# An mLSTM and two expert layers on one core: the first phase in finer steps and a new order of its first 520

## The chip, the cores and the metric

The program runs on one core of a Trainium2 chip. The metric is the device time in microseconds (us) of one execution; lower is better. The engines are TensorE (PE in the rows; PEld is its weight load), VectorE (DVE), ScalarE (ACT), GpSimd (POOL) and SyncE (SP), which issues nearly all DMAs from one queue in order.

## The reference

```python
for t in range(S):                      # attention: B, H, S, D = 4, 8, 768, 40
    m_new = max(f_gate + m, i_gate)
    f_stab, i_stab = exp(f_gate + m - m_new), exp(i_gate - m_new)
    C = f_stab * C + i_stab * outer(v, k)
    n = f_stab * n + i_stab * k
    y = sigmoid(o_gate) * (C @ q) / max(abs(n . q), 1)
h = x @ w_in                            # x: 3072 x 320, w_in: 320 x 2048
x = (max(h, 0) + alpha * min(h, 0)) @ w_out
e = argmax(x @ w_gate)                  # 8 experts, 320 -> 1024 -> 320
out = prob[e] * sigmoid(x @ w_output_gate)[e] * relu(x @ w1[e]) @ w2[e]
```

## The kernel before

The recurrence is computed in chunks of 128 tokens: 24 units u (4 batches of 6 chunks). For each unit `load_g`, `att_e`, `att_s` build the decayed scores, `att_h` the part from the running state, `att_b` the sum over values, `att_y` the normalised and gated output y, `att_c` its transpose into the FFN's input `xT`, and `prep_kt` and `att_d` update the state. Three units make one block of 384 tokens, and the dense FFN goes over 8 blocks with 16 chunks of 128 hidden columns each: `ffn1` k (eight matmuls of 384 columns into the PSUM tile `ph`, then ScalarE's `v` and VectorE's scaled sum), `ffn_split` k (the activation as a high part on ScalarE and the rest `gl` on VectorE, into the tile `ring`), `ffn2` k (nine matmuls of 336 columns into `acc`). `block_out` reads `acc` after the sixteenth.

All matmul operands are kept in two parts, a rounded high part and the rest. So the weights are decoded and split at the start: `load_wi`, `dec_wi` (three VectorE instructions, L614 to L618, that put 64-bit words together as float32), `split_wi` (L630 on ScalarE, L631), and `load_wo`, `dec_wo`, `split_wo` (L647, L648) likewise, 16 of each; `gate_w` and `gate_w2` multiply `w_out` by the router's weights with small matmuls (`pw`, `pwg`). `gates` makes the gate prefix sums `G` of a part of the sequence in nine VectorE instructions and stores them to the DRAM tensor `gd`, from which `load_g` broadcasts them back as `D`; `gates_e` and `gates_d` turn them into factors (`pe_ek`, `pe_dec`). `expert_load`, `expert_split` and `expert_store` prepare the experts' weights for the second layer, which runs from about 500 us on.

Everything up to the second layer stands in one written order: the string ORDER has a code for each step (F is `ffn1`, g `ffn_split`, S `ffn2`, as `att_s`, and so on; STEPS maps them), and each engine's queue gets the instructions as the steps come. No scheduler changes this afterwards, and an engine whose next instruction waits holds all behind it. The table OTHER says for which numbers of a step the elementwise instruction goes to the other of VectorE and GpSimd: `engine(usual, other, name, i)`. ORDER also has 20 `warm` steps, each one 512-column matmul on zeros whose result nothing reads (L1172).

PSUM tiles come from three tags: `att` (3 buffers, attention and `pw`, `pwg`), `acc` (3) and `hps` (2, the `ph` tiles). `v` comes from a pool with 2 buffers.

Of the kernel before, what the change touches and what calls it, by code (L numbers as in the profile page):

```python
# [8 lines left out]
F32 = mybir.dt.float32  # L9
# [8 lines left out]
P = 128  # L18
# [25 lines left out]
KR = 64 + D  # L44

OTHER = {
    "prep_kt": (
        1, 3, 4, 7, 8, 9, 13, 14, 15, 16,  # L50
    ),
    "att_y": (
        0, 1, 2, 4, 7, 11, 13, 16, 17, 18, 19, 20, 21, 22, 23,
    ),
    "expert_split": (
        0, 1, 2, 3, 5, 6, 7, 8, 10, 12, 13, 14, 15, 18, 19, 20, 25, 26, 27, 30, 31, 32, 33, 34, 35, 36,
        37, 38, 39, 40, 41, 42, 43, 44, 45, 46, 47, 48, 49, 50, 51, 52, 53, 54, 55, 56, 57, 58, 59, 60,
        61, 62, 63,
    ),
    "split_wi": (  # L60
        0, 1, 3, 5, 13, 14,
    ),
    "split_wo": (
        2, 4, 10, 15,
# [5 lines left out]
for _n, _w in (  # L70
# [11 lines left out]
lo load_gates do load_cst load_gates lo lo gates do gates_e lq gates gates_e do do warm ah so load_g ae gw do do so  # L82
do do gw load_wg load_sel li gates_d gates_d lv pt lv di di di si gv gv do lo do do do load_g ae as lg ad so so log
sg li li gw gw lq li di di di di load_g ab ay pt ay load_g di load_gates si ah ay ay di si ad ae di di di ac lo do
warm warm si load_g load_g do gv ae as ae lo lq do do do do warm ab ay so so ay ay gv ay gw warm lo lo lo warm warm
warm lg gw do ae do do do so as do lv ac gv lq lq ah gates ab set_al1 gv ay gw lo do do gw warm warm so li pt do
warm lg warm warm gates_e do so load_g ay ay ay warm do do gates_d gw di do di warm warm di lv ac warm warm warm ad
pt si el load_g es li di di lo gv gv F di load_g F g et ah si ae do g lo do do ae S F gw as so so load_g warm g S
gw do do li di log do so ae li di ad di lv gv gv F gw di di di ae F as lg load_g ah si lo si g do do ae g S S lg lg
li do so di ab ay ay ay pt di el es lq gw di li di log F F di di et g g ad si pt li di li di di si di di sg gv lo  # L90
lq sg si el S S load_g ay F F g S di ah do lv ab si do load_g do es li et F g gv li lv ay ac ay lo ay ay di g S S
ae ae di as so gw di di di F F ab di g g si li lv ac load_g di ay si S di load_g load_g li gv do di S ay el do ay
do ay F gv ae si F g di di S ae S pt lg lo g lq lq di as el ae si ad so ad pt F ac load_g do g do do ab ay ay S so
gw gw es ah log ay et ay F gv gv g lg es F g as S ah F F g ab et load_g S ae g load_g ae ay ay ay el ad bo el el es
es F F lg load_g ae S ac load_g lv ae S pt et g S g es ah lq lv ad F ay g F S as lq ah F et ab ay S g g ac el ay et
es lv el F F as S g es load_g ae lg lg et ay lq ay S sg S et g F ab ay load_g bp lg S g ac S pt el ad F F S g g S
el el es lq es F g F g ay ay ay ah pt S pt S et es F S et g F log ad g ae et as ae S bo F g F load_g ae ab ay el lv
el S g ay es el F as g load_g load_g es et es et F load_g ac lv ah el el ae ae lg lg S g S S F g ad pt ah ay es F g
ab F ay ad et ae et S g el load_g el F es ay et F ay ay ac S g es ae S g ah F S S et es ay et g lv el el bp as F F
el g es et pt S S ab ac g ad F F g S g ay lq sg es es S ay lv pt F ay el lq g F as S g F et es ah ad S log S g bo F  # L100
sg et g load_g load_g ay el el F lg S ae ab ay ay ay et S F S g lq lq S g ae ac lg el S as lv load_g load_g load_g
es et es et ay F pt F g g ab ae ay ac F S g es ay ay ay S F F ae as lq S g g load_g ah ad ac ae el F lv pt el ae g
et ab ay ay S es es F et et g load_g ay F S g as ay lv S load_g S F g F ah ab ay S el el es ad lg ay ae g ay el es
# [12 lines left out]
first_s first_tl route_c2 first_t first_tl first_s first_2 first_2 route_d first_st first_2 first_2
# [19 lines left out]
    "di": ("dec_wi", [(i, j) for i in range(16) for j in range(3)]),  # L136
    "gates_e": ("gates_e", zip(range(3))),
# [12 lines left out]
    "warm": ("warm", zip(range(20))),  # L150
# [31 lines left out]
def mlstm_moe_kernel(  # L182
# [262 lines left out]
    with ExitStack() as p1:  # L445
# [70 lines left out]
        def gates(part):  # L516
            c0, c1, o = GPARTS[part]
            nn, n = c1 - c0, (c1 - c0) * P
            fs = slice(c0 * P, c1 * P)
# [3 lines left out]
            gx[part] = GG, w  # L523
# [5 lines left out]
            V.tensor_tensor(g[:, 1:], tf[:, 1:], m[:, : n - 1], ALU.add)  # L529
            lo = 1 if part == 0 else 0  # L530
            V.tensor_tensor(g[:, lo:], g[:, lo:], m[:, lo:], ALU.subtract)
            V.tensor_copy(mlast, m[:, n - 1 : n])
            for c in range(nn):
                cs = slice(c * P, (c + 1) * P)
                V.tensor_tensor_scan(GG[:, cs], onesP[:GR], g[:, cs], 0.0, ALU.mult, ALU.add)
            V.tensor_tensor(w, ti, m, ALU.subtract)
            V.tensor_tensor(w, w, GG, ALU.subtract)
            nc.sync.dma_start(gd[:, fs], GG[: B * H])

        def gates_e(part):  # L540
            c0, c1, o = GPARTS[part]
            nn, n = c1 - c0, (c1 - c0) * P
            GG, w = gx[part]
            V.tensor_tensor(
# [105 lines left out]
        def gate_w(i):  # L650
# [3 lines left out]
            for k in range(3):  # L654
                c0 = min(k * P, DM - P)
                T.transpose(pt[:, k * P : (k + 1) * P], f[:, c0 : c0 + P], ident)
# [666 lines left out]
```

## Time and profile before

| | |
|---|---|
| median of 3 runs | 784.55 us (780.52 to 784.94) |
| the profiled execution | 782.92 us |
| its span, first to last instruction | 781.1 us |
| TensorE, VectorE, ScalarE, GpSimd busy | 751.7, 472.0, 363.2, 164.9 us |
| mean granted TensorE clock | 0.99 |

The profile is of one execution. Times are counted from the span's start. A matmul's end is modelled, so a busy TensorE need not be one at its peak; the distance between the starts of two matmuls is measured. TensorE's matmuls of float32 operands run in two passes, which the rows count as two instructions.

### The profile page before, as it was taken

The numbers are of one execution on the slowest core, as the hardware profiler recorded it, in microseconds if no ns is written. First come the engines' busy times: TensorE is split into PE (matmuls) and PEld (weight loads), VectorE is DVE, ScalarE is ACT, GpSimd is POOL, SyncE is SP. The second block draws the span as 40 slices with busy tenths as digits, with TensorE's granted clock in tenths as the row PEclk, the third lists the DMA queues.
The fourth block names the chain that finished last, engine by engine and source line by source line (L and its number), as shares of the span: only waits on it lengthen the run. The fifth ranks groups of instructions, "written<-read, shape, count | busy, mean of one in ns | idle before, by whom it ended". The sixth has DMA issues, their size and how long they took to land. (4 is left out here: it accounts for less than half of the span.)

```text
span 781.1 us, 15245 instructions
## 1 busy us (share of the span) xinstructions
PE 751.7 (96%) x4931; PEld 714.8 (92%) x4931; DVE 472.0 (60%) x1159; ACT 363.2 (47%) x810; POOL 164.9 (21%) x225
## 2 busy tenths in 40 slices
PE   2899999999999999999999999999999999999995
PEld 2787999989999999999999999998999999999994
DVE  4878998775767566767687786867332232232231
ACT  3536666636664654655565354433333233233231
POOL 1222433203130323210000000012232232232232
PEclk9988999999999999999999999999999999999998
DMA  6938877876788785766977868795977645921000
GB/s 194 258 111 262 271 243 231 258 234 242 230 283 296 236 294 179 234 234 245 307 255 257 294 240 303 274 340 189 383 305 292 240 171 201 428 83 39 29 22 13
DMA packets 81787, 179.64 MB, mean 230 GB/s; under 512 B 8700, under 2 KB 39481, under 8 KB 80428
## 3 DMA queue, kind: packets, MB, share of 16 engines
q1 hardware_dynamic: 78252, 169.92, 63.4%
q0 software_dynamic: 3456, 8.71, 3.3%
q8 instruction: 45, 0.74, 0.4%
q14 instruction: 34, 0.28, 0.1%
HBM read 246.55 MB, written 55.59 MB: 387 GB/s over the span
## 5 line engine op out<-in xcount | busy, mean ns | idle before, releaser
L834 PE MATMUL ph<-ring 128*128 128x384 f32 x1024 | 196.7, 340 | 0.0
L834 PEld LDWEIGHTS ph<-ring 128*128 128x128 f32 x1024 | 177.0, 188 | 1.8 <-DVE ring L850 0.4
L862 PE MATMUL acc<-ring 128*128 128x336 f32 x384 | 123.4, 326 | 0.5 <-ACT ring L849 0.5
L863 PE MATMUL acc<-ring 128*128 128x336 f32 x384 | 119.6, 317 | 0.0
L842 ACT ACTIVATE v<-ph 128x384 f32<-128x384 f32 x128 | 62.3, 489 | 114.5 <-PE ph L834 114.2
L843 DVE SCALAR_TENSOR_TENSOR ph<-v,al,ph 128x384 f32<-128x384 f32 x128 | 78.3, 618 | 53.2 <-ACT v L842 52.8
L409 DVE TENSOR_SCALAR yo<-po,xg 128x320 f32<-128x320 f32 x26 | 14.3, 551 | 137.3 <-PE po L289 137.3
L289 PE MATMUL po<-ring,hh 128*128 (+1 forms) x432 | 95.6, 308 | 0.0
L289 PE MATMUL p<-ring,xh 128*128 (+1 forms) x324 | 89.9, 398 | 0.0
L850 DVE TENSOR_TENSOR ring<-ph,ring 128x384 fp32r<-128x384 f32 x128 | 70.3, 553 | 31.4 <-ACT ring L849 29.7
L849 ACT ACTIVATE ring<-ph 128x384 fp32r<-128x384 f32 x128 | 62.1, 488 | 52.9 <-DVE ph L843 43.4
L865 PE MATMUL acc<-ring 128*128 128x336 f32 x384 | 80.2, 317 | 0.0
L289 PEld LDWEIGHTS po<-ring,hh 128*128 128x128 f32 x432 | 73.2, 187 | 2.3 <-ACT hh L389 0.2
L862 PEld LDWEIGHTS acc<-ring 128*128 128x128 f32 x384 | 72.3, 188 | 1.9 <-ACT ring L849 0.9
L863 PEld LDWEIGHTS acc<-ring 128*128 128x128 f32 x384 | 72.3, 188 | 0.0
L389 ACT ACTIVATE hh<-p 128x512 fp32r<-128x512 f32 x54 | 29.4, 595 | 86.5 <-PE p L387 86.5
L289 PEld LDWEIGHTS p<-ring,xh 128*128 128x128 f32 x324 | 58.8, 188 | 11.3
L289 PE MATMUL po<-ring,hl 128*128 (+1 forms) x216 | 66.5, 308 | 0.2 <-DVE hl L391 0.2
L376 ACT ACTIVATE hr<-p 128x512 f32<-128x512 f32 x56 | 33.4, 597 | 67.3 <-PE p L289 63.7
L865 PEld LDWEIGHTS acc<-ring 128*128 128x128 f32 x384 | 63.5, 189 | 0.2 <-DVE ring L850 0.2
L700 ACT ACTIVATE D<-D,EKT 128x128 f32<-128x128 f32 x192 | 60.7, 393 | 3.5 <-DMA D<-gd 3.3
L410 POOL DMA_INDIRECT out_dram<-yo,tok x28 | 28.1, 1003 | 160.8 <-DVE yo L409 146.2
(197 smaller groups left out, 1139.6 us busy)
## 6 DMA issues: line engine op xcount, KB each, us to landing
ring<-scr SPq DMA_DIRECT2D x26, 3072.0 KB
ring<-scr SPq DMA_DIRECT2D x26, 2560.0 KB
ring<-scr SPq DMA_DIRECT2D x33, 512.0 KB
D<-gd SPq DMA_DIRECT2D x48, 256.0 KB
er<-in_ew_dram SPq DMA_DIRECT2D x32, 384.0 KB
scr<-ring SPq DMA_DIRECT2D x32, 384.0 KB
scr<-er SPq DMA_DIRECT2D x32, 384.0 KB
er<-in_ew_dram SPq DMA_DIRECT2D x32, 320.0 KB
```

Of the source, the lines that this page charges most:

```text
L289: mm = T.matmul(o_, lhsT, r, start=start, stop=stop)
L376: A.activation(hr_half(j, hf), ph, AF.Relu)
L389: A.activation(hh[:, hs], pts[j, hf], AF.Copy)
L700: A.activation(d[:, j], d[:, j], AF.Exp, bias=EKT[:, c, i + j : i + j + 1])
L834: T.matmul(ph[:, :384], wi_[i][lo][:, wc], xTs[n % 2][:, xc], start=(a == 0), stop=(a == len(PASSES) - 1),)
L842: A.activation(v, ph[:, :384], AF.Relu, scale=-1.0)
L843: V.scalar_tensor_tensor(ph[:, :384], v, al1[:, i : i + 1], ph[:, :384], ALU.mult, ALU.add)
L849: A.activation(gh, v, AF.Copy)
L850: V.tensor_tensor(gl, v, gh.bitcast(F32), ALU.subtract)
L862: T.matmul(ac, gh[:, sl], hi, start=(i == 0), stop=False)
L863: T.matmul(ac, gh[:, sl], lo, start=False, stop=False)
L865: T.matmul(accs[n][t][:, :NO], gl[:, t * P : (t + 1) * P], hi, start=False, stop=(i == NFC - 1))
```

## The change

Steps that issued matmuls and the instructions that empty their result are cut in two: `att_s` and `att_m`, `att_h` and `att_n`, `att_d` and `att_u`, `att_b` and `att_a`, `att_c` and `att_x`, `gate_w` and `gate_c`, `gate_w2` and `gate_s`, `ffn1` and `ffn_act`; `gates` is cut into `gates`, `gates_g`, `gates_st` (the store) and `gates_w`. The first 520 steps of the new ORDER, up to the first `block_out`, are a new order of the same steps as the first 443 before; behind it the order is the old one with both halves of a step side by side. No `warm` step is left. For k below 24, `ffn_act` writes its sum over `v` in SBUF and not into `ph`, and 12 of those `ffn_split` run their subtraction on GpSimd. OTHER changes for some others.

```diff
+KEEP = 24
 OTHER = {
+    "ffn_split": (
+        0, 1, 3, 4, 5, 6, 7, 9, 15, 17, 20, 22,
+    ),
     "prep_kt": (
-        1, 3, 4, 7, 8, 9, 13, 14, 15, 16,
+        0, 1, 2, 3, 4, 7, 8, 9, 13, 14, 15, 16,
     "att_y": (
-        0, 1, 2, 4, 7, 11, 13, 16, 17, 18, 19, 20, 21, 22, 23,
+        3, 4, 6, 7, 11, 13, 16, 17, 18, 19, 20, 21, 22, 23,
     "expert_split": (
-        0, 1, 2, 3, 5, 6, 7, 8, 10, 12, 13, 14, 15, 18, 19, 20, 25, 26, 27, 30, 31, 32, 33, 34, 35, 36,
+        0, 2, 3, 5, 6, 7, 8, 10, 12, 13, 14, 15, 18, 19, 20, 25, 26, 27, 30, 31, 32, 33, 34, 35, 36, 37,
...
+    "gates_w": (
+        0, 2,
+    ),
     "split_wi": (
-        0, 1, 3, 5, 13, 14,
+        1, 5, 6, 7, 8, 9, 11, 13, 14,
     "split_wo": (
-        2, 4, 10, 15,
+        1, 3, 5, 6, 8, 9, 11, 13, 14, 15,
 ORDER = """
-lo load_gates do load_cst load_gates lo lo gates do gates_e lq gates gates_e do do warm ah so load_g ae gw do do so
+lo do lo do do do do load_gates load_cst gw so gc do lo gw gates gates_g load_gates gates_w gates_e load_wg lv do
...
-es F F lg load_g ae S ac load_g lv ae S pt et g S g es ah lq lv ad F ay g F S as lq ah F et ab ay S g g ac el ay et
+F f F f lg load_g ae S ac ax load_g lv ae S pt et g S g es ah an lq lv ad au F f ay g F f S as am lq ah an F f et
...
-    "warm": ("warm", zip(range(20))),
+    "warm": ("warm", zip(range(200))),
...
             V.tensor_tensor(g[:, 1:], tf[:, 1:], m[:, : n - 1], ALU.add)
+            V.tensor_copy(mlast, m[:, n - 1 : n])
+            gx[part] = GG, w, g, m
+
+        def gates_g(part):
...
             V.tensor_tensor(g[:, lo:], g[:, lo:], m[:, lo:], ALU.subtract)
-            V.tensor_copy(mlast, m[:, n - 1 : n])
             for c in range(nn):
                 cs = slice(c * P, (c + 1) * P)
                 V.tensor_tensor_scan(GG[:, cs], onesP[:GR], g[:, cs], 0.0, ALU.mult, ALU.add)
-            V.tensor_tensor(w, ti, m, ALU.subtract)
-            V.tensor_tensor(w, w, GG, ALU.subtract)
-            nc.sync.dma_start(gd[:, fs], GG[: B * H])
+
+        def gates_st(part):
+            c0, c1, o = GPARTS[part]
+            nc.sync.dma_start(gd[:, c0 * P : c1 * P], gx[part][0][: B * H])
+
+        def gates_w(part):
...
+            eng = engine(V, G, "gates_w", part)
+            eng.tensor_tensor(w, ti, m, ALU.subtract)
+            eng.tensor_tensor(w, w, GG, ALU.subtract)
...
                     T.matmul(pp[hf][:, j * P : (j + 1) * P], qk[r, HH + j], qk[r, j], start=True, stop=True)
+            t["pp"] = pp
+
+        def att_m(u):
+            t = ut[u]
+            pp = t["pp"]
             for hf in range(2):
                 d = t["D", hf].rearrange("p h t -> p (h t)")
                 V.tensor_tensor(d, pp[hf], d, ALU.mult)
...
+            gt[k] = ph
+
+        def ffn_act(k):
+            ph = gt[k]
+            i = k % NFC
             v = hp.tile([P, 384], F32, tag="v", bufs=2, name=f"v_{k}")
             A.activation(v, ph[:, :384], AF.Relu, scale=-1.0)
-            V.scalar_tensor_tensor(ph[:, :384], v, al1[:, i : i + 1], ph[:, :384], ALU.mult, ALU.add)
-            gt[k] = ph[:, :384]
+            g = v if k < KEEP else ph[:, :384]
+            V.scalar_tensor_tensor(g, v, al1[:, i : i + 1], ph[:, :384], ALU.mult, ALU.add)
+            gt[k] = g
...
             A.activation(gh, v, AF.Copy)
-            V.tensor_tensor(gl, v, gh.bitcast(F32), ALU.subtract)
+            engine(V, G, "ffn_split", k).tensor_tensor(gl, v, gh.bitcast(F32), ALU.subtract)
```

TensorE just ahead of the first `ffn1`, before. `pw` and `pwg` are the router products, `pt` the transpose of a unit's output, `pd` the state update, `ph` the FFN; a number behind a name is that of the tile.

```order
L656 MATMUL pw_567<-cst,f_wo_478 128x128 x3
L1172 MATMUL warm_573<-ring 128x512
L1172 MATMUL warm_575<-ring 128x512
L1172 MATMUL warm_583<-ring 128x512
L1172 MATMUL warm_587<-ring 128x512
L1172 MATMUL warm_589<-ring 128x512
L554 MATMUL pe_ek_594<-cst,w_525 128x96 x3
L1172 MATMUL warm_610<-ring 128x512
L572 MATMUL pe_dec_616<-gin,sel 120x12 x3
```

The same place on TensorE now, up to the first three `ffn1`.

```order
L592 MATMUL pe_ek_569<-cst,w_412 128x96 x3
L610 MATMUL pe_dec_580<-gin,sel 120x12 x3
L693 MATMUL pw_602<-cst,f_wo_553 128x128 x3
L693 MATMUL pw_608<-cst,f_wo_575 128x128 x3
L913 MATMUL ph_617<-ring 128x384 x8
L808 MATMUL pd_626<-kv_2_398,kt 120x123 x3
L693 MATMUL pw_635<-cst,f_wo_631 128x128 x3
L913 MATMUL ph_646<-ring 128x384 x8
L706 MATMUL pwg_663<-wgt,woT_591 128x16 x3
L808 MATMUL pd_673<-kv_3_500,kt 120x123 x3
L913 MATMUL ph_677<-ring 128x384 x8
```

No warm matmul stands between the factors and the FFN any more; one `pd` and two `pwg` that stood ahead of the first `ph` stand behind it, and the first three `ph` are no longer two together.

VectorE at the prefix sums of part 2 of the gates, before.

```order
L735 TENSOR_TENSOR hN_520<-pb_516,EKT 128x328
L524 SCALAR_TENSOR_TENSOR m_522<-gin,mlast 96x384
L528 TENSOR_TENSOR g_524<-gin,mlast 96x1
L529 TENSOR_TENSOR g_524<-gin,m_522 96x383
L531 TENSOR_TENSOR g_524<-g_524,m_522 96x384
L532 COPY mlast<-m_522 96x1
L535 SCALAR_TENSOR_TENSOR G_523<-cst,g_524 96x128 x3
L536 TENSOR_TENSOR w_525<-gin,m_522 96x384
L537 TENSOR_TENSOR w_525<-w_525,G_523 96x384
```

The end of the same place on VectorE now; the part's first scan, `m_409`, stands twenty rows ahead of L560.

```order
L764 TENSOR_TENSOR D_0_394<-ps_0_469,D_0_394 128x512
L764 TENSOR_TENSOR D_1_396<-ps_1_470,D_1_396 128x512
L652 TENSOR_SCALAR f_wo_502<-r_wo_405 128x320
L654 SCALAR_TENSOR_TENSOR f_wo_502<-r_wo_405,f_wo_502 128x320
L686 TENSOR_TENSOR ring<-f_wo_420,ring 128x320
L560 TENSOR_TENSOR g_411<-g_411,m_409 96x384
L563 SCALAR_TENSOR_TENSOR G_410<-cst,g_411 96x128 x3
L656 SCALAR_TENSOR_TENSOR f_wo_502<-r_wo_405,f_wo_502 128x320
L859 TENSOR_TENSOR pa_491<-pa_491,hN_380 128x328
```

Score products, decoding and a `wo` split now stand inside the gate chain, and the two subtractions into `w` have left VectorE.

GpSimd at the first FFN chunks, before.

```order
L678 TENSOR_TENSOR kt<-kv_3_638,EKT 128x320
L631 TENSOR_TENSOR ring<-f_wi_629,ring 128x384
L701 AFFINE_SELECT D_0_602<-D_0_602 128x512
L701 AFFINE_SELECT D_1_666<-D_1_666 128x512
L648 TENSOR_TENSOR ring<-f_wo_612,ring 128x320
```

The same place on GpSimd now.

```order
L724 TENSOR_TENSOR kt<-kv_2_398,EKT 128x320
L724 TENSOR_TENSOR kt<-kv_3_500,EKT 128x320
L669 TENSOR_TENSOR ring<-f_wi_641,ring 128x384
L935 TENSOR_TENSOR ring<-v_660,ring 128x384
L747 AFFINE_SELECT D_0_587<-D_0_587 128x512
L747 AFFINE_SELECT D_1_589<-D_1_589 128x512
L686 TENSOR_TENSOR ring<-f_wo_686,ring 128x320
L935 TENSOR_TENSOR ring<-v_690,ring 128x384
```

The L935 rows are the `gl` subtractions of the first two FFN chunks, which stood on VectorE before.

## Rows read from the trace of the kernel before

**Rows 1.** The page: busy time of each engine, share of the span, instructions
```profile
PE 751.7 (96%) x4931; PEld 714.8 (92%) x4931; DVE 472.0 (60%) x1159; ACT 363.2 (47%) x810; POOL 164.9 (21%) x225
```
**Rows 2.** Busy time by stretch; then clock, DMA share, GB/s
```profile
0.00:71.50 71.50, 53.39 (x265) 46.77 (x266) 51.57 (x143) 29.40 (x73) 15.44 (x26) 0.93 0.69 199
71.50:150.70 79.20, 78.53 (x580) 75.45 (x579) 69.48 (x162) 51.23 (x129) 27.75 (x35) 1.00 0.79 252
150.70:760.00 609.30, 607.70 (x4018) 581.81 (x4018) 346.39 (x848) 279.48 (x603) 116.20 (x159) 1.00 0.68 238
```
**Rows 3.** Waits of VectorE, 0 to 71.5 us: total, times, longest
```profile
DVE f_wo L614 <- DMA r_wo<-in_wo_dram: 3.9, 1, 3.9
DVE DEC L580 <- PE pe_dec L572: 2.4, 2, 1.5
DVE G L535 <- DMA cst<-in_consts_dram: 1.9, 1, 1.9
DVE D L713 <- PE ps L710: 1.6, 2, 1.2
DVE pa L788 <- PE pa L778: 1.4, 1, 1.4
DVE dn L797 <- PE pa L778: 1.4, 1, 1.4
```
**Rows 4.** SyncE in order of time, around 50 us: start, duration, issue
```profile
44.62 1.55 SPq L478 DMA_DIRECT2D q<-in_qs_dram  x4
57.38 0.31 SPq L538 DMA_DIRECT2D gd<-G  x1
```
**Rows 5.** Busy time by stretch (columns of rows 2), 50 to 70 us
```profile
50.00:60.00 10.00, 9.24 (x56) 8.37 (x53) 8.89 (x25) 2.47 (x8) 1.46 (x2) 0.63 0.17 54
60.00:70.00 10.00, 9.46 (x56) 7.78 (x55) 8.58 (x25) 5.15 (x12) 3.59 (x5) 0.86 0.88 257
```
**Rows 6.** TensorE in order of time: start, duration, matmuls of one line
```profile
41.14 3.58 PE L778 MATMUL pa<-kv,D 128*128 128x41 f32 x16
...
60.15 2.48 PE L1172 MATMUL warm<-ring 128*128 128x512 f32 x5
...
68.47 3.04 PE L834 MATMUL ph<-ring 128*128 128x384 f32 x16
...
89.32 1.87 PE L778 MATMUL pa<-kv,D 128*128 128x41 f32 x16
...
91.31 3.04 PE L834 MATMUL ph<-ring 128*128 128x384 f32 x16
94.19 0.80 PE L750 MATMUL pd<-kv,kt 128*120 128x123 f32 x6
```
**Rows 7.** VectorE and GpSimd by line, 0 to 150.7 us: busy, mean ns, idle before
```profile
L1101 DVE TENSOR_TENSOR er<-er,ring 128x768 fp32r<-128x768 f32 x4 | 3.8, 952 | 1.0 <-ACT ring L1100 1.0
L631 DVE TENSOR_TENSOR ring<-f_wi,ring 128x384 fp32r<-128x384 f32 x6 | 3.3, 552 | 0.9 <-ACT ring L630 0.9
L648 DVE TENSOR_TENSOR ring<-f_wo,ring 128x320 fp32r<-128x320 f32 x4 | 2.2, 539 | 0.3 <-ACT ring L647 0.3
L678 DVE TENSOR_TENSOR kt<-kv,EKT 128x320 f32<-128x320 f32 x3 | 1.9, 632 | 0.8 <-DMA kv<-in_kv_dram 0.8
L537 DVE TENSOR_TENSOR w<-w,G 96x384 f32<-96x384 f32 x1 | 0.6, 553 | 0.0
...
L631 POOL TENSOR_TENSOR ring<-f_wi,ring 128x384 fp32r<-128x384 f32 x10 | 10.1, 1014 | 13.2 <-ACT ring L630 13.2
```
**Rows 8.** TensorE by line, 0 to 71.5 us
```profile
L1172 PE MATMUL warm<-ring 128*128 128x512 f32 x19 | 9.5, 612 | 0.0
```
**Rows 9.** VectorE, then GpSimd, in order of time near 106 us
```profile
106.40 1.03 DVE L616 SCALAR_TENSOR_TENSOR f_wo<-r_wo,f_wo 128x320 int32<-128x320 int32 x1
107.47 0.49 DVE L618 SCALAR_TENSOR_TENSOR f_wo<-r_wo,f_wo 128x320 int32<-128x320 int32 x1
...
106.07 1.01 POOL L631 TENSOR_TENSOR ring<-f_wi,ring 128x384 fp32r<-128x384 f32 x1 [1.51 <-ACT ring L630]
```

More of the change, by code (lines that the diff above doesn't have):

```diff
@@ L81 @@
 ORDER = """
-lo load_gates do load_cst load_gates lo lo gates do gates_e lq gates gates_e do do warm ah so load_g ae gw do do so
[L83 to L91, printed above, removed]
@@ L136 @@
     "di": ("dec_wi", [(i, j) for i in range(16) for j in range(3)]),
+    "f": ("ffn_act", zip(range(128))),
+    "am": ("att_m", zip(range(24))),
+    "an": ("att_n", zip(range(24))),
+    "au": ("att_u", zip(range(24))),
+    "aa": ("att_a", zip(range(24))),
+    "ax": ("att_x", zip(range(24))),
+    "gc": ("gate_c", zip(range(16))),
+    "gs": ("gate_s", zip(range(16))),
+    "gates_g": ("gates_g", zip(range(3))),
+    "gates_st": ("gates_st", zip(range(3))),
+    "gates_w": ("gates_w", zip(range(3))),
     "gates_e": ("gates_e", zip(range(3))),
@@ L529, in gates @@
             V.tensor_tensor(g[:, 1:], tf[:, 1:], m[:, : n - 1], ALU.add)
+            V.tensor_copy(mlast, m[:, n - 1 : n])
+            gx[part] = GG, w, g, m
+        def gates_g(part):
+            c0, c1, o = GPARTS[part]
+            nn, n = c1 - c0, (c1 - c0) * P
+            GG, w, g, m = gx[part]
             lo = 1 if part == 0 else 0
             V.tensor_tensor(g[:, lo:], g[:, lo:], m[:, lo:], ALU.subtract)
-            V.tensor_copy(mlast, m[:, n - 1 : n])
             for c in range(nn):
@@ L535, in gates @@
                 V.tensor_tensor_scan(GG[:, cs], onesP[:GR], g[:, cs], 0.0, ALU.mult, ALU.add)
-            V.tensor_tensor(w, ti, m, ALU.subtract)
-            V.tensor_tensor(w, w, GG, ALU.subtract)
-            nc.sync.dma_start(gd[:, fs], GG[: B * H])
+        def gates_st(part):
+            c0, c1, o = GPARTS[part]
+            nc.sync.dma_start(gd[:, c0 * P : c1 * P], gx[part][0][: B * H])
+        def gates_w(part):
+            c0, c1, o = GPARTS[part]
+            nn, n = c1 - c0, (c1 - c0) * P
+            GG, w, g, m = gx[part]
+            ti = gin[:GR, 0, o : o + n]
+            eng = engine(V, G, "gates_w", part)
+            eng.tensor_tensor(w, ti, m, ALU.subtract)
+            eng.tensor_tensor(w, w, GG, ALU.subtract)
         def gates_e(part):
@@ L542, in gates_e @@
             nn, n = c1 - c0, (c1 - c0) * P
-            GG, w = gx[part]
+            GG, w = gx[part][:2]
             V.tensor_tensor(
@@ L561, in gates_d @@
                 return
-            GG, w = gx[part]
+            GG, w = gx[part][:2]
             dec = gin[:32, 0, o : o + B * nn].rearrange("p (b c) -> p b c", b=B)
@@ L652, in gate_w @@
             pt = ps_att(f"pw_{i}")
-            w = hp.tile([P, XW], F32, tag="xr", bufs=3, name=f"woT_{i}")
             for k in range(3):
@@ L656, in gate_w, with gate_c @@
                 T.transpose(pt[:, k * P : (k + 1) * P], f[:, c0 : c0 + P], ident)
+            woT[i] = pt
+        def gate_c(i):
+            pt = woT[i]
+            w = hp.tile([P, XW], F32, tag="xr", bufs=3, name=f"woT_{i}")
             A.activation(w[:, : 3 * P], pt[:, : 3 * P], AF.Copy)
@@ L664, in gate_w2, with gate_s @@
                 T.matmul(pw[:, : 2 * E], w[:, k * P : (k + 1) * P], wgt[:, k], start=(k == 0), stop=(k == 2))
+            woT[i] = pw
+        def gate_s(i):
+            pw = woT[i]
             hi, lo = wo_[i]
@@ L733, in att_h, with att_n @@
                     )
+                t["pb"] = pb
+        def att_n(u):
+            b, c = divmod(u, NC)
+            t = ut[u]
+            if c > 0:
+                pb = t["pb"]
                 t["hN"] = hN = rp.tile([P, H, 41], F32, tag="hN", bufs=2, name=f"hN_{u}")
@@ L756, in att_d, with att_u @@
                     )
+                t["pd"] = pdl
+        def att_u(u):
+            b, c = divmod(u, NC)
+            t = ut[u]
+            if c < NC - 1:
+                pdl = t["pd"]
                 if c == 0:
@@ L784, in att_b, with att_a @@
                 )
+            t["pa0"] = pa
+        def att_a(u):
+            b, c = divmod(u, NC)
+            t = ut[u]
+            pa = t["pa0"]
             if c > 0:
@@ L819, in att_c, with att_x @@
                 T.transpose(pt[:, k * P : (k + 1) * P], t["y"][:, k * P : (k + 1) * P], ident)
+            t["pt"] = pt
+        def att_x(u):
+            t = ut[u]
+            n = u // 3
+            xT = xTs[n % 2]
+            cols = slice((u % 3) * P, (u % 3 + 1) * P)
+            pt = t["pt"]
             pv = pt[:, :384].rearrange("p (k t) -> p k t", k=3)
```

69 lines of the change are left out of this document (41 added, 28 removed).

## Prediction

> **What bounds the kernel now.** I read the busy shares first, then the busy time by stretch, then the waits inside the first stretch, then TensorE's order of time. TensorE is busy 751.7 of 781.1 us [rows 1]. By stretch the picture differs: from the first `block_out` at 150.7 us to 760 us TensorE is busy 607.7 of 609.3 us, from 71.5 to 150.7 us it is busy 78.53 of 79.20, and ahead of 71.5 us, where VectorE starts the first FFN activation, only 53.39 of 71.50 [rows 2]. So after 71.5 us the end is set by how much work TensorE has left, and whatever arrives earlier there ends earlier by as much. The change rewrites the order up to the first `block_out` and leaves the rest as it was, so everything is decided in the two stretches that end at 150.7 us.
>
> The first stretch is bound by no single engine. VectorE is busy 51.57 us of it and idle 19.9. Of the idle time 3.9 us is the landing of the first weights and 1.9 us that of the constants; 2.4 + 1.6 + 1.4 + 1.4 = 6.8 us are waits for matmuls that the same step had only just issued [rows 3]. The DMA queue has a hole too: after 46.2 us SyncE issues nothing until the gate prefix sums of part 2 exist at 57.4 us [rows 4], and the DMA share falls to 0.17 between 50 and 60 us [rows 5].
>
> TensorE is slow there as well. The clock row says nothing against full speed before 50 us, but sixteen passes of `att_b` take 3.58 us at 41.14 us and 1.87 us at 89.32 us [rows 6]. A ratio of 1.9 is 1.2 against 2.4 GHz, so I take TensorE to run at 1.2 GHz nearly up to 50 us. The row of 50 to 60 us has 0.63, that of 60 to 70 us 0.86: 2.8 us more at half speed, so the clock is up for good at about 62.8 us. Just ahead of that stand five warm matmuls, 2.48 us [rows 5, 6].
>
> **The change, part by part.** The base is the profiled execution: 782.9 us, span 781.1, so 1.8 us lie around the span. It is 1.6 us under the median of the three runs, 784.55.
>
> *Work taken off VectorE ahead of the first activation.* Counting instructions in the two orders up to that point: two `kt` products go to GpSimd (2 x 0.63), four gate subtractions go there (two long ones at 0.55, two short ones at about half that: 1.6 in all), three gated `y` products (3 x 0.54, taken from the 320-column row) and one expert split of 768 columns (0.95). Two `wi` splits (2 x 0.55) and two instructions of one decode (at most 1.1) are put off until after the first activation, as are two 16-column instructions (0.3). Four `wo` splits come the other way (4 x 0.54 = 2.2). The sum is 1.3 + 1.6 + 1.6 + 0.95 + 1.1 + 1.1 + 0.3 - 2.2 = 5.7 us [rows 7]. Neighbours on VectorE overlap a little, so I count 5 us. GpSimd hides what it gets: it is busy 15.44 of 71.5 us [rows 2].
>
> *TensorE ahead of the first FFN matmul.* Nineteen of the twenty warm matmuls stand there, 9.5 us of TensorE [rows 8]; they all go. One `att_d` and two `gate_w2` move behind it; six passes take 0.80 us at full speed [rows 6], so 1.4 us or so each at half, 4 us. Against that, the full speed that followed the warm matmuls, for a little while up to 52.6 us (0.63 of the clock in 50 to 60 us means 7.4 us at half) and from 62.8 to 68.5 us, goes with them [rows 5]; I put the other work in it at 7 us, which would take twice as long, 7 us more. The balance is 9.5 + 4 - 7 = 6.5 us earlier. Both engines thus reach the first FFN matmul about 5 us sooner if each wait stays as it is. Term one: -5 us, between 0 (another wait takes over) and -6.5.
>
> *Waits.* A step used to issue a matmul and at once the instruction that empties it, so VectorE's queue stood still in between. Now the two are separate steps with other work in front of the second. It can take away at most the 19.9 - 3.9 - 1.9 = 14.1 us that are not landings, and at least nothing; the rows that name a matmul as the cause hold 6.8 us [rows 3]. I take -5 us, three quarters of those. The split store of the prefix sums helps little: SyncE still meets it behind a like number of loads, and the sums come only as much earlier as VectorE's work in front of them shrinks, some 4 us.
>
> *The second stretch.* TensorE has 0.7 us to spare in it [rows 2]. The deferred matmuls add 1.8 us at full speed, and one warm matmul goes. With no warm matmul ahead, the first two `ffn1`, 2.88 us at full speed [rows 6], probably run at half: 2.9 us more. That is 4.5 us against a reserve of 0.7: between +0.9 (the clock is up in time) and +3.8. I take +2.5.
>
> *Activations kept in SBUF.* For k below 24 the scaled sum is written over `v` and the PSUM bank is free one step earlier; 12 of the `gl` subtractions go to GpSimd, ten of them ahead of the first `block_out`, 1.01 us each by the `wi` row against 0.55 on VectorE [rows 7]. On VectorE, 69.48 of 79.20 us busy in the second stretch, 5.5 us go and the deferred 2.5 us come: nothing on the path while TensorE is full. The sum written to SBUF is not in the trace; between a subtraction within SBUF (0.55) and the `kt` product (0.63) it differs from today's by less than 0.1 us, 1.5 us over all 19 either way on VectorE, and I take no difference. `v` has two buffers and is now held until its `gl` is done: `ffn_act` k+2 on ScalarE waits for that, with the copies behind it in ScalarE's queue. The order has `ffn_split` k ahead of `ffn_act` k+2 for every k, by 7 steps at least, so I count nothing; without that cover each wait would cost up to 1 us of a queue that is busy 51.23 of 79.20 us [rows 2].
>
> *VectorE against GpSimd.* At 106.40 us a two-input VectorE instruction takes 1.03 us and ends only after the GpSimd subtraction that started at 106.07 has ended; the next of the same kind takes 0.49 [rows 9]. So the two do exclude each other now and then. The nine `gl` that stay on VectorE there read two SBUF operands now instead of one, and GpSimd gets some 10 us more work: I allow 0 to +3 us on VectorE, not on the path, and take nothing.
> The Trainium skill (SBUF — State Buffer, "Who interferes with whom") says that a VectorE instruction with two SBUF inputs contends with a GpSimd instruction that reads SBUF, and that the later one blocks until the first is done. The trace agrees at this place. By that rule alone each of the nine could lose up to a GpSimd instruction of 1.01 us, 9 us of VectorE at worst; it speaks against keeping `v` in SBUF, but against the 9.7 us that VectorE has free there and the 3 us net that it is relieved of, the sum above would not move.
>
> Sum: -5 - 5 + 2.5 = -7.5 us. From 782.9 that is 775.4; from the median it would be 777.0. I say 776.
>
> **Rivals.**
> *More of the waits go.* If the order lets VectorE run through (14.1 us instead of 5) and the second stretch costs only 0.9: -5 - 14.1 + 0.9 = -18.2 us, 765. For it: the waits are many and short, and the work to put between is there. Against it: of TensorE's 53.39 us in the first stretch 9.5 are warm matmuls, so over 40 remain, all at half speed now [rows 2, 8], and the first landings stay.
> *The waits only move.* Half-speed TensorE is late for every separated step, VectorE waits elsewhere: waits 0, term one -5, second stretch +3.8: -1.2, 782. For it: TensorE is busy 9.24 and 9.46 us of the 10 between 50 and 60 and between 60 and 70 us already [rows 5].
> *The clock stays low.* The place is the start of the FFN. If the first two `ffn1`, spread among small matmuls now, do not bring 2.4 GHz and TensorE stays at 1.2 until the seventh, it has about 24 us of full-speed work in that stretch (an estimate: six `ffn1` at 1.44, four `ffn2` of like length, and ten smaller steps of 0.3 to 1.9) and pays that again, less the 0.7 of reserve: -5 - 5 + 1.6 + 23 = +15, 798. It turns slower than before from the fourth `ffn1` on, where the loss passes 10 us. For it: before, the clock fell at about 52.6 us although TensorE was 92% busy between 50 and 60 us, and rose behind warm matmuls [rows 5, 6]. Against it: two `ffn1` occupy TensorE longer than those five warm matmuls did.
> The Trainium skill (TensorE: Matmul & The Clock Gate, "What's actually happening") calls the low clock the default that activity releases; the row of 60 to 70 us, with the rise behind the warm matmuls, agrees [rows 5].
>
> **How the numbers follow.** Forecast (771 to 781) 0.44; more of the waits 0.20; only moved 0.23; clock low 0.13. A measurement can tell about 1% from no change, so faster means under 776.7 us. Half of the forecast and all of the first rival lie under it, with a little of the second: 0.46. Slower by over 1% means above 792.4: most of the last rival, 0.12. The rest, 0.42, lies within 1%. The range reaches from 764, which takes in the first rival, to 788, which takes in the second and a clock that comes up one or two `ffn1` late.
>
> **What would show it.** Right: the first `ffn1` starts near 60 us instead of 68.5 and the first `block_out` near 143 instead of 150.7; VectorE's waits for `pe_dec`, `ps` and `pa` are short; the first two `ffn1` take about 5.8 us instead of 2.9, the later ones 2.9. From there on the distance to the end stays 630 us. Wrong: a granted clock of 0.5 beyond the third `ffn1`; a first `block_out` after 150 us; VectorE waiting for GpSimd's `gl`, or TensorE's `ffn2` for it; or a second stretch much longer than 82 us.

## The result and the profile after

| | before | after |
|---|---|---|
| median of 6 runs each on one chip, us | 784.44 (780.52 to 784.94) | 776.32 (774.72 to 779.46) |
| ratio to before, 95% interval | | 0.9912 (0.9884 to 0.994) |
| the profiled execution, its span, us | 782.92, 781.1 | 776.72, 775.0 |
| first `ffn1` starts, us | 68.47 | 56.56 |
| VectorE's first activation, us | 71.5 | 62.1 |
| first `block_out`, us | 150.7 | 143.7 |

The change saves 0.9%. All of it is won ahead of the first `block_out`: 7.0 us there, and from there to the end the distance is 630.4 us before and 631.3 after. The page of the kernel after first (columns of [rows 1]): TensorE has 20 instructions less and 1.9 us less to do, GpSimd 15.2 us more.

```profile
PE 749.8 (97%) x4911; PEld 714.4 (92%) x4911; DVE 471.4 (61%) x1148; ACT 364.9 (47%) x812; POOL 180.1 (23%) x236
```

Busy time by stretch of the kernel after, cut at the same events as [rows 2]: the start of the first activation and the first `block_out`.

```profile
0.00:62.10 62.10, 49.40 (x234) 44.67 (x235) 48.76 (x131) 28.79 (x71) 22.29 (x34) 1.00 0.78 228
62.10:143.70 81.60, 80.33 (x592) 77.39 (x592) 72.46 (x166) 53.72 (x133) 32.99 (x37) 1.00 0.79 243
143.70:754.00 610.30, 608.13 (x4016) 581.62 (x4016) 345.73 (x846) 279.39 (x603) 119.44 (x161) 1.00 0.67 238
```

The first stretch is 9.4 us shorter: VectorE has 2.8 us less to do in it (48.76 against 51.57) and stands idle for 13.3 us and not 19.9. The second is 2.4 us longer, and TensorE is still busy in all but 1.3 us of it. The third stays TensorE's, so the gain is carried to the end.

Waits of VectorE up to 62.1 us after (total, times, longest), the answer to [rows 3].

```profile
DVE f_wo L652 <- DMA r_wo<-in_wo_dram: 4.3, 2, 3.8
DVE DEC L618 <- PE pe_dec L610: 2.9, 2, 1.5
DVE f_wi L652 <- DMA r_wi<-in_wi_dram: 2.0, 1, 2.0
...
DVE state L823 <- PE pd L808: 0.6, 1, 0.6
DVE pd L826 <- PE pd L808: 0.6, 1, 0.6
...
DVE D L764 <- PE ps L756: 0.2, 1, 0.2
```

The same view of before has three more waits for TensorE, behind those of [rows 3]:

```profile
DVE state L758 <- PE pd L750: 0.6, 1, 0.6
...
DVE f_wo L614 <- PE pw L656: 0.5, 1, 0.5
...
DVE hN L735 <- PE pb L727: 0.2, 1, 0.2
```

The waits for `pa` and `dn` are gone, `ps` is down from 1.6 to 0.2 us, `pd` is up from 0.6 to 1.2. `pe_dec`, whose matmul and copy stand in `gates_d` and were not cut apart, costs 2.9 and not 2.4. All waits for TensorE together fell from 8.1 to 4.3 us.

SyncE after around the store of the prefix sums (start, duration, issue), the answer to [rows 4].

```profile
40.84 0.35 SPq L635 DMA_DIRECT2D r_wo<-in_wo_dram  x1
47.70 0.33 SPq L635 DMA_DIRECT2D r_wo<-in_wo_dram  x1
...
49.04 0.38 SPq L567 DMA_DIRECT2D gd<-G  x1
```

The store goes out at 49.04 us and not at 57.38. The hole of 11.2 us ahead of it is now one of 6.5 us (41.2 to 47.7) and one of 3.3 us behind the store, up to the next load at 52.67. The DMA share of 50 to 60 us is 0.76 where it was 0.17, that of the first stretch 0.78 where it was 0.69.

TensorE after in order of time (columns of [rows 6]).

```profile
37.02 3.48 PE L843 MATMUL pa<-kv,D 128*128 128x41 f32 x16
...
56.56 2.91 PE L913 MATMUL ph<-ring 128*128 128x384 f32 x8
59.27 1.43 PE L808 MATMUL pd<-kv,kt 128*120 128x123 f32 x6
60.49 0.56 PE L693 MATMUL pw<-cst,f_wo 128*128 128x128 f32 x3
60.80 1.65 PE L913 MATMUL ph<-ring 128*128 128x384 f32 x8
62.29 0.74 PE L706 MATMUL pwg<-wgt,woT 128*128 128x16 f32 x6
...
77.57 1.93 PE L843 MATMUL pa<-kv,D 128*128 128x41 f32 x16
```

The first `ffn1` and the `pd` behind it take 59.27 - 56.56 = 2.71 and 1.22 us from start to start: half speed. The second `ffn1` takes 62.29 - 60.80 = 1.49 us, the full 2.4 GHz. So full speed begins between these two, after the first `ffn1`, and the granted clock is 1.00 in the stretches behind it. Ahead of it the clock column shows 1.00 too, though the sixteen passes of `pa` take 3.48 us at 37 us and 1.93 at 77 us: there the speed has to be read from the passes.

### The profile page after: what moved, and what is told of

It is laid out like the page before. It is cut to its first block, busy times and chain, and to the rows that moved or that the text cites. A ratio compares the mean times of both kernels' runs of the same rounds, so it can differ in the third digit from the quotient of the medians.

```text
span 775.0 us, 15190 instructions
## 1 busy us (share of the span) xinstructions
PE 749.8 (97%) x4911; PEld 714.4 (92%) x4911; DVE 471.4 (61%) x1148; ACT 364.9 (47%) x812; POOL 180.1 (23%) x236
## 4 chain that ended last, share of the span: by engine, by line
PE 84%; DVE 7%; DMA 4%; ACT 2%; issue 1%; POOL 0%; SPq 0%; POOLq 0%; DVEq 0%; ACTq 0%
PE ph L913 21%; PE po L313 13%; PE p L313 13%; PE acc L947 7%; PE acc L948 7%; PE acc L950 7%; PE pa L843 4%; PE ps L756 3%; PE p L411 3%; DMA r_wi<-in_wi_dram 2%; PE pd L808 2%; PE pb L778 1%; PE xt L373 1%; PE pt L890 1%; DMA er<-in_ew_dram 1%
## 5 line engine op out<-in xcount | busy, mean ns | idle before, releaser
L913 PE MATMUL ph<-ring 128*128 128x384 f32 x1024 | 198.7, 343 | 0.0
L928 DVE SCALAR_TENSOR_TENSOR ph<-v,al,ph 128x384 f32<-128x384 f32 x104 | 63.8, 618 | 49.5 <-ACT v L926 49.2
L935 DVE TENSOR_TENSOR ring<-ph,ring 128x384 fp32r<-128x384 f32 x104 | 57.3, 554 | 29.0 <-ACT ring L934 28.0
L934 ACT ACTIVATE ring<-ph 128x384 fp32r<-128x384 f32 x104 | 50.5, 488 | 43.6 <-DVE ph L928 37.4
```

The costliest lines, as they stand in the source:

```text
L913: T.matmul(ph[:, :384], wi_[i][lo][:, wc], xTs[n % 2][:, xc], start=(a == 0), stop=(a == len(PASSES) - 1),)
L928: V.scalar_tensor_tensor(g, v, al1[:, i : i + 1], ph[:, :384], ALU.mult, ALU.add)
L934: A.activation(gh, v, AF.Copy)
L935: engine(V, G, "ffn_split", k).tensor_tensor(gl, v, gh.bitcast(F32), ALU.subtract)
```

## The experiments

Each ratio is to the kernel before, run on the same chip. The question behind all of them: does one part of the change carry the gain, and what becomes of the others without it. Stretches are those of one profiled execution each; the kernel before alone ranges from 780.25 to 786.1 us, so a difference of 1 or 2 us between two stretches says little.

**The warm matmuls alone.** Before, with the 20 `warm` steps taken out of ORDER.

```diff
-lo lo do ... do do warm ah so load_g ae gw do do so
+lo lo do ... do do ah so load_g ae gw do do so
```

> The kernel before without its 20 warm matmuls, nothing else. Theory (the new order and the moved work make the gain; the warm matmuls go at no net gain, since the full speed that follows them goes too): first ffn1 between 65 and 70 us, first block_out between 149 and 154 us, time between 782 and 787 us. Rival (TensorE's 9.5 us of warm matmuls were the gain): first ffn1 below 62 us, time below 779 us.

Measured: 785.37 us, 1.0034 (1.002 to 1.0047). The first `ffn1` starts at 69.66 us, 1.2 us later than before, and the first pair takes 4.31 us from start to start, where [rows 6] has 2.88 at 91.31 us:

```profile
69.66 4.46 PE L834 MATMUL ph<-ring 128*128 128x384 f32 x16
73.97 0.83 PE L727 MATMUL pb<-state,qg 120*128 120x123 f32 x6
```

That fits one of the two at half speed and one at full (2.88 + 1.44). So the 9.5 us of warm matmuls, gone alone, give nothing back. TensorE waited at other places instead, and their clock was missing for about one `ffn1`.

**The old shares of VectorE and GpSimd in the new order.** After, with the table of before for `prep_kt`, `att_y`, `expert_split`, `split_wi`, `split_wo`, and `gates_w` on VectorE; the list for `ffn_split` stays.

```diff
     "split_wi": (
-        1, 5, 6, 7, 8, 9, 11, 13, 14,
+        0, 1, 3, 5, 13, 14,
     "split_wo": (
-        1, 3, 5, 6, 8, 9, 11, 13, 14, 15,
+        2, 4, 10, 15,
...
```

> The changed kernel with the old shares of VectorE and GpSimd for kt, y, the expert, wi and wo splits and the gate subtractions; the order, the cut steps, the kept activations and their split on GpSimd stay. Theory (some 5 us of VectorE work ahead of the first ffn1 is one of two parts of the gain): first ffn1 between 59 and 62 us instead of 56.6, first block_out 3 to 5 us after 143.7, time between 779 and 782 us. Rival (the order alone does it, VectorE is not the bound there): first ffn1 below 58 us, time between 775 and 778 us.

Measured: 786.08 us, 1.0039 (1.0023 to 1.0055): the whole gain is lost, more than either theory gave. The first `ffn1` is only 2.4 us late (58.92); the rest is lost in the second stretch, 94.6 us against 87.1 from the first `ffn1` to `block_out`. Its busy times, and what VectorE waits for in it:

```profile
58.90:153.50 94.60, 88.57 (x618) 84.83 (x616) 76.36 (x168) 56.21 (x138) 40.82 (x48) 0.98 0.71 224
```
```profile
DVE ring L932 <- ACT ring L931: 5.4, 3, 2.4
DVE f_wi L649 <- POOL ring L666: 3.9, 2, 2.3
```

GpSimd has 40.8 us of work there, against 34.5 in the kernel after, and VectorE's decoding waits for its splits. TensorE is idle for 6.0 us, against 1.3. The new order fits the new shares and not the old ones.

**The activations kept in SBUF.** Nine `ffn1` k+2 stand ahead of `ffn_split` k in the new order, which two PSUM banks allow only if the activation has left its bank. The first kernel moves these nine behind their `ffn_split` and keeps the rest of the change; the second does the same, with no activation kept and all `gl` on VectorE.

```diff
-f gv si di di di ad F do gs f el ah au g S ae ...
+f gv si di di di ad do gs f el ah au g F S ae ...
```
```diff
-KEEP = 24
+KEEP = 0
-    "ffn_split": (
-        0, 1, 3, 4, 5, 6, 7, 9, 15, 17, 20, 22,
-    ),
```

> The changed kernel with nine ffn1 k+2 moved behind ffn_split k in the order; all else stays. It is the control for the next. Theory: TensorE is full after the first ffn1 and finds its work in another sequence: within 2 us of 776. Rival (running ahead by two PSUM tiles is what the kept activations are for): 778 to 782 us.

> The order of the control, but no activation kept in SBUF, and so all gl subtractions on VectorE. Theory (VectorE has some 10 us free in the second stretch, TensorE sets it): 0 to 3 us over the control. Rival (the freed PSUM tile and the 5.5 us taken off VectorE are a main part): 4 us or more over the control, first block_out beyond 148 us.

Measured: 780.66 us, 0.9982 (0.9966 to 0.9999), for the moves alone, and 793.92 us, 1.0155 (1.0122 to 1.0188), for the second. The control itself is 4.3 us slower than the kernel after, as its rival said: the nine `ffn1` that run ahead are worth something. Stretches from the first `ffn1` to the first `block_out`, the first kernel and then the second:

```profile
56.20:147.60 91.40, 87.66 (x616) 84.48 (x615) 79.14 (x176) 56.02 (x138) 33.06 (x39) 0.96 0.74 234
```
```profile
55.30:160.20 104.90, 92.51 (x618) 87.44 (x616) 79.52 (x187) 55.60 (x138) 23.22 (x29) 0.93 0.67 207
```

TensorE stands idle 12.4 us in the second, against 3.7 in the first, and is busy 4.9 us longer at the lower granted clock (0.93 against 0.96). The largest of its waits there is new:

```profile
PE ph L910 <- DVE ring L932: 7.9, 6, 2.4
```

The next `ffn1` waits for the `gl` that reads its bank. Keeping the activations, with their split between two engines, is worth 13 us in this order.

**All `gl` on VectorE, and all on GpSimd,** in the kernel after; activations stay kept. The edit for VectorE; for GpSimd the list holds all of 0 to 23.

```diff
-    "ffn_split": (
-        0, 1, 3, 4, 5, 6, 7, 9, 15, 17, 20, 22,
-    ),
```

> The changed kernel with all gl subtractions on VectorE; the activations below 24 stay in SBUF. Theory (what the kept activations give is the PSUM tile that comes free early, and VectorE still has room): PSUM waits of ffn1 stay away, VectorE busy 5 us more in the second stretch, time between 777 and 782 us. Rival (the share of GpSimd is the main part): 786 us or more.

> The changed kernel with all 24 gl subtractions of the kept activations on GpSimd instead of 12. Theory (each gl on GpSimd takes 0.55 us off VectorE, but 1.08 us of GpSimd and a chance to shut VectorE out): time between 774 and 781 us. Rival (VectorE bounds the second stretch): 5 us less of it there, time below 774 us.

Measured: 780.76 us, 0.9965 (0.9945 to 0.9984), on VectorE, and 778.88 us, 0.9938 (0.9914 to 0.9961), on GpSimd; the share of the kernel after, 0.9912, is the best of the three by its middle, though the last two intervals overlap. The same stretch, first on VectorE, then on GpSimd:

```profile
56.40:147.80 91.40, 88.63 (x618) 84.94 (x616) 80.73 (x187) 56.05 (x138) 22.97 (x29) 0.98 0.76 232
```
```profile
56.00:145.00 89.00, 86.75 (x611) 83.20 (x610) 77.97 (x168) 56.28 (x138) 44.54 (x48) 0.98 0.74 235
```

So of the 13 us some 4 belong to the share (780.76 - 776.32), and by difference about 9 to the bank, if the share is worth as much in the order of the control; the bank alone was not run in one order with one share.

**The same in the old order.** Before, with KEEP and the list for `ffn_split`.

```diff
-            V.scalar_tensor_tensor(ph[:, :384], v, al1[:, i : i + 1], ph[:, :384], ALU.mult, ALU.add)
+            g = v if k < KEEP else ph[:, :384]
+            V.scalar_tensor_tensor(g, v, al1[:, i : i + 1], ph[:, :384], ALU.mult, ALU.add)
...
```

> The kernel before with only the kept activations and the same 12 gl subtractions on GpSimd; old order, old steps, warm matmuls stay. Theory (in the old order ffn1 k+2 stands behind ffn_split k anyway, so an early free PSUM tile is of no use): between 781 and 785 us, as before. Rival (the kept activations help in any order, as the loss without them suggests): below 778 us.

Measured: 784.59 us, 1.0024 (1.0005 to 1.0044). In an order that has every `ffn_split` k ahead of `ffn1` k+2 the freed bank, with 12 `gl` on GpSimd, is worth nothing; TensorE has little idle time there to win, 1.6 us:

```profile
66.10:149.70 83.60, 82.00 (x597) 78.48 (x597) 73.64 (x159) 53.00 (x133) 40.32 (x46) 1.00 0.75 247
```

**All but the order.** Before, with all of the new table, KEEP and `gates_w`'s choice of engine; the old steps and order, and the warm matmuls, stay.

```diff
+KEEP = 24
-        0, 1, 3, 5, 13, 14,
+        1, 5, 6, 7, 8, 9, 11, 13, 14,
-        2, 4, 10, 15,
+        1, 3, 5, 6, 8, 9, 11, 13, 14, 15,
...
```

> The kernel before with all of the change but the order and the cut steps: its shares of VectorE and GpSimd, the gate subtractions among them, and the kept activations; the 20 warm matmuls stay. Theory (VectorE's relief is worth something only where the order fills its waits): first ffn1 2 to 4 us sooner than 68.5, first block_out 0 to 3 us sooner, time between 780 and 785 us. Rival (the work moved to GpSimd makes the gain in any order): time below 779 us.

Measured: 795.34 us, 1.0163 (1.0135 to 1.0192), outside both ranges: the shares without the order make it slower. The first `ffn1` starts at 74.6 us, the first `block_out` at 161.2. VectorE's largest wait up to there:

```profile
DVE ring L656 <- ACT ring L655: 8.4, 4, 3.3
```

VectorE waits for ScalarE at the `wo` splits that it has got. Some of its instructions take longer too: the `wi` split averages 711 ns where it took 552 before [rows 7]. The single instructions (shortest, median, longest, in ns) show what that mean is made of:

```profile
L639 DVE TENSOR_TENSOR ring<-f_wi,ring x9: 542/551/1026, 31.0 to 134.4; 128x384 fp32r<-128x384 f32 x9
```

The median does not move; a few instructions take nearly twice as long. A mean of six or nine such instructions is a poor witness for the longer GpSimd lists: in the kernel before without its warm matmuls, with the old lists, it is 632. A count of all is a better one. Up to the first `block_out` 27 VectorE instructions take over 0.1 us more than the median of their kind, 12.8 us more in sum; before it is 9 with 3.5 us, without the warm matmuls 6 with 2.4, and with kept activations and 12 `gl` moved (the run above) 19 with 9.4. Every one of them starts while a GpSimd instruction runs.

**The separation alone.** After, with the separated pairs up to the first `block_out` closed where the buffers allow it: the step that empties a tile is moved up towards its matmuls; the rest of the order stays. By the two ORDER strings 80 of the 89 pairs stand apart in the kernel after and 32 here; the text below says 54 closed, by the strings it is 48.

```diff
-lo do lo do do do do load_gates load_cst gw so gc do lo gw gates ...
+lo do lo do do do do load_gates load_cst gw gc so do lo gw gc gates ...
```

> The changed kernel with 54 of the cut steps of its first 520 closed again: the instruction that empties a matmul stands right behind it, where the other buffers allow that; the matmuls keep their places, tables and kept activations stay. Theory (the cut is what took VectorE's waits for matmuls away): VectorE's waits for TensorE ahead of the first ffn1 back at 6 us or more (2.9 + 0.6 + 0.2 in the changed kernel), first ffn1 between 60 and 67 us, time between 781 and 792 us. Rival (the sequence of the steps made the gain, not the cut): first ffn1 within 2 us of 56.6, time between 774 and 779 us.

Measured: 825.49 us, 1.055 (1.052 to 1.058), far outside both ranges. The first `ffn1` starts at 71.98 us, the first `block_out` at 190.2. From 76 us to the first `block_out` TensorE is idle 18.3 of 114 us, and its granted clock is 0.88:

```profile
76.00:190.00 114.00, 95.71 (x595) 88.96 (x595) 79.43 (x175) 55.01 (x135) 32.84 (x38) 0.88 0.58 180
```

VectorE's waits up to 80 us, then TensorE's up to 190 us:

```profile
DVE hN L793 <- PE pb L778: 3.9, 1, 3.9
...
DVE pa L859 <- PE pa L843: 3.3, 1, 3.3
```
```profile
PE pw L693 <- DVE f_wo L656: 8.6, 4, 3.3
PE pe_ek L592 <- ACT w L589: 7.6, 3, 3.3
```

VectorE waits for the matmul, and then the next matmul for VectorE. In this order the separation is worth 49 us, a part of which is the lower clock: from the first `ffn1` to `block_out` TensorE is busy 99.9 us with the work that takes 85.8 in the kernel after. This is not a price of closed pairs in general, since the old order has all pairs closed and needs 784 us.

**Warm matmuls again.** After, with six `warm` ahead of the first `ffn1`; and after, with 76, twelve at the start and two behind each step of TensorE up to the first `ffn1`.

```diff
-... so so gw gc gw gc pt lo F ad pt do
+... so so gw gc gw gc pt lo warm warm warm warm warm warm F ad pt do
```
```diff
-lo do lo do do do do load_gates load_cst gw so gc ...
+warm warm warm warm warm warm warm warm warm warm warm warm lo do lo do do do do load_gates load_cst gw warm warm so gc ...
```

> The changed kernel with six warm matmuls put back ahead of the first ffn1. Theory (only the first ffn1 runs at half speed, some 2 us, and six warm matmuls at half speed take 2.6 us): first ffn1 between 58 and 60 us with its eight passes in 1.5 us, first block_out between 143 and 146 us, time between 775 and 779 us. Rival (the cold start of the FFN is what the second stretch lost): first block_out below 142 us, time below 774 us.

> The changed kernel with 76 warm matmuls: twelve at the start, where TensorE waits for the first landings, and two behind each of its steps up to the first ffn1. Theory (VectorE's 44 us of work and the landings bound the first stretch as much as TensorE at half speed does): TensorE at full speed from about 10 us on, first ffn1 between 53 and 57 us, first block_out 2 to 5 us sooner, time between 771 and 775 us. Rival A (TensorE at half speed alone sets the first ffn1): first ffn1 below 51 us, time below 770 us. Rival B (the warm matmuls stand in the way, or do not hold the clock): first ffn1 above 58 us, time above 778 us.

Measured: 777.67 us, 0.9942 (0.9919 to 0.9965), with six, and 781.8 us, 0.9984 (0.9961 to 1.0008), with 76. TensorE with six:

```profile
56.15 2.91 PE L1258 MATMUL warm<-ring 128*128 128x512 f32 x6
58.85 2.26 PE L914 MATMUL ph<-ring 128*128 128x384 f32 x8
60.95 0.80 PE L809 MATMUL pd<-kv,kt 128*120 128x123 f32 x6
```

The six take 2.70 us, and the first `ffn1` behind them is still partly slow: 2.10 us from start to start, not the 1.5 expected, against 2.71 without them. The first `block_out` stands at 143.8 us as without them. With 76, four stretches near the start:

```profile
10.00:20.00 10.00, 8.60 (x52) 6.38 (x52) 7.93 (x25) 4.76 (x15) 2.54 (x3) 1.00 0.77 227
20.00:30.00 10.00, 9.96 (x45) 8.53 (x44) 6.73 (x18) 6.78 (x16) 3.39 (x4) 0.51 1.00 307
30.00:40.00 10.00, 10.00 (x65) 8.66 (x64) 7.76 (x19) 4.23 (x9) 3.71 (x5) 0.80 0.67 204
40.00:50.00 10.00, 8.34 (x61) 6.51 (x60) 9.69 (x25) 3.98 (x12) 5.09 (x7) 1.00 0.43 140
```
The granted clock falls to 0.51, half speed, while TensorE is busy 9.96 of 10 us, and in two of the four it is at 1.00 (at 45.71 us the sixteen passes of `pa` take 1.87 us, full speed). The first `ffn1` runs at full speed, but starts at 60.65 us, 4.1 us later than without them, as rival B said. The extra matmuls take TensorE's time (it is idle for 6.3 us up to the first `ffn1`, where it was 12.7) and lift its clock only in parts; what a faster TensorE without them would bring to the first stretch stays open.

## Why the prediction came out right

The forecast was 776, the measurement 776.3. Step by step it holds less well than that.

*What bounds it.* Right. The first `block_out` is 7.0 us sooner, the span 6.1 us shorter, and nothing behind it made the difference up.

*Term one, -5 us.* Right for TensorE, too large for VectorE. Up to the first `ffn1` TensorE has 43.86 us to do where it had 50.36, the 6.5 us of the prediction. VectorE's busy time up to the first activation fell by 2.8 us. The instructions that went and came were counted rightly: at their times of before they are worth some 5.0 us. But others got longer, by 2.2 us. Counted as above, six VectorE instructions of this stretch take over 0.1 us more than the median of their kind, 2.5 us more in sum, where it was two with 0.5 us before, and each starts while a GpSimd instruction runs. Ten decoding instructions of `wo` before, and the same ten after (shortest, median, longest):

```profile
L616 DVE SCALAR_TENSOR_TENSOR f_wo<-r_wo,f_wo x10: 481/492/534, 8.3 to 63.2; 128x320 int32<-128x320 int32 x10
```
```profile
L654 DVE SCALAR_TENSOR_TENSOR f_wo<-r_wo,f_wo x10: 480/492/1189, 4.2 to 57.4; 128x320 int32<-128x320 int32 x10
```

The median is the same, and the longest has more than doubled. It starts while GpSimd does one of the gate subtractions that the change gave it, and ends 0.36 us after it:

```profile
44.16 1.19 DVE L654 SCALAR_TENSOR_TENSOR f_wo<-r_wo,f_wo 128x320 int32<-128x320 int32 x1
```
```profile
43.88 1.11 POOL L575 TENSOR_TENSOR w<-gin,m 96x384 f32<-96x384 f32 x1
```

Behind the first activation the same happens to the splits and to `gl`, which now reads two operands from SBUF (before, one of them was in PSUM):

```profile
L850 DVE TENSOR_TENSOR ring<-ph,ring x19: 544/547/559, 73.0 to 148.4; 128x384 fp32r<-128x384 f32 x19
```
```profile
L935 DVE TENSOR_TENSOR ring<-v,ring x9: 539/554/1014, 73.7 to 141.3; 128x384 fp32r<-128x384 f32 x9
```

In that stretch twelve such instructions lose 5.0 us, where seven lost 3.0 before: 2.0 us more, inside the 0 to +3 that the prediction allowed. What failed in "VectorE against GpSimd, not on the path, take nothing" is the place: the price was allowed for the second stretch only, and 2.0 us more of it fell into the first, where VectorE's work counts. The Trainium skill (SBUF — State Buffer, "Who interferes with whom") has a VectorE instruction with two SBUF inputs and a GpSimd instruction that reads SBUF contend, the later one blocked until the first is done; the trace agrees with the pair at 44 us, 1.19 us against a median of 0.49.

VectorE's second stretch was also counted short. The new lists give it three `wi` and two `wo` splits more there, which the "3 us net that it is relieved of" leaves out: its busy time went from 69.48 to 72.46 us. TensorE is full there, so this cost nothing.

*Waits, -5 us.* Near in size, by other parts: 6.6 us of idle time went, but only 3.8 of them were waits for TensorE (8.1 to 4.3). The others were waits for ScalarE and GpSimd and 1.0 us of landings. `ps`, `pa` and `dn` went as foreseen. `pe_dec`, 2.4 of the 6.8 us that the prediction wanted to shorten, could not, for its step was not cut: the diff leaves `gates_d` alone. That the separation takes such waits away was seen from the other side: with most pairs closed, waits for `pb` and `pa` of 3.9 and 3.3 us appear. "The split store of the prefix sums helps little, some 4 us" was mis-sized: it goes out 8.3 us sooner.

The two terms together were -10 for the first stretch, and -9.4 was measured. That the sum holds is luck: work gave 2.2 us less than foreseen and waits 1.6 more.

*The second stretch, +2.5 us.* It is +2.4, by other parts. Half speed took one `ffn1` and not two, and this falls ahead of the first activation, so that none of the 2.9 us is in the +2.4. It is 1.8 us more of TensorE's work (80.33 against 78.53) and 0.6 us more idle (1.27 against 0.67). That 1.8 is also the figure that was counted for three deferred steps is in part chance: two of them lie in this stretch (60 passes of `pwg` against 48), the `pd` does not (24 in both).

*Activations kept, "count nothing".* The step failed, with no effect on the sum. The cover that it named holds for ScalarE's queue; but the gain is at TensorE, where the bank comes free earlier. In the old order it is nothing. In the new one, with the nine `ffn1` moved back, it is 13 us together with the share on GpSimd, and without both the kernel is slower than before; the nine that run ahead, which the freed bank allows, are worth 4.3 us more. The sum came out right because the order was priced as a whole.

*The rivals.* The clock that stays low fell: from the second `ffn1` on, at 60.80 us, TensorE is at full speed. The waits that only move fell too, for the order as it is; something like it happens where a part is missing, with closed pairs most of all. "More of the waits go" was not reached: 13.3 us of idle time are left, of which 4.3 + 2.0 are waits for weights to land.

None of the parts that were tried alone gains: without warm matmuls 1.0034, with kept activations 1.0024, with all shares 1.0163 in the old order; in the new one 1.0039 with the old shares, 1.0155 with no activation kept, 1.055 with closed pairs. So the gain belongs to order, cut steps, shares and kept activations together, as far as these runs show. What was not tried is the new order with none of the other parts, an order of the same kind without the kept activations, laid out for itself, or one with `pe_dec` cut apart.

## What to carry to other kernels

An order written out for in-order queues is good only for the shares and buffers for which it was laid out: price and test such a change as a whole, and do not read the worth of a part from taking it away, which here was 4 to 49 us for parts of a change that saves 8. When work moves from VectorE to GpSimd, look at what then runs beside it on VectorE: most instructions keep their time, but one that falls upon a GpSimd instruction can take twice as long, 0.2 to 0.7 us more in each of the six ahead of the first activation. Extra matmuls to lift the clock gave nothing in this order (six) or cost 5.5 us (76).

## What was not expected of the hardware

The exclusion of VectorE and GpSimd lengthens both. GpSimd's ten `gl` average 1132 ns after, where the like-sized `wi` split takes 1014 before [rows 7] and 1021 after. One of them starts while VectorE decodes with two operands from SBUF, and takes 1.30 us; another, beside VectorE instructions with at most one operand from SBUF, takes 1.01:

```profile
77.39 0.58 DVE L656 SCALAR_TENSOR_TENSOR f_wi<-r_wi,f_wi 128x384 int32<-128x384 int32 x1
```
```profile
77.53 1.30 POOL L935 TENSOR_TENSOR ring<-v,ring 128x384 fp32r<-128x384 f32 x1
79.17 1.01 POOL L935 TENSOR_TENSOR ring<-v,ring 128x384 fp32r<-128x384 f32 x1 [0.35 <-POOL ring L935]
```

And the granted clock fell to half in a stretch in which TensorE was busy 9.96 of 10 us with small matmuls and `warm` ones, and stood at full in one with 8.34: the busy time of a stretch did not tell its clock here.
